# An RWKV-5 attention into a soft mixture of experts: K, R and V transposed as pairs of tokens, a shorter maximum, a reordered tail

## The chip, the cores and the metric

One core of one Trainium2 chip runs the whole program. The time is the device time of one execution, in microseconds (us). The kernel before took 127.64 us (median of 3 runs, 126.82 to 129.72).

## The reference

```python
B, H, S, D = 4, 8, 768, 48          # r, k, v: [B, H, S, D] fp32; w, u: [H, D]
for t in range(S):                  # attention with a decaying state
    cur   = einsum('bhd,bhe->bhde', u * k_t, v_t)
    y_t   = einsum('bhd,bhde->bhe', r_t, state + cur)
    state = w * state + einsum('bhd,bhe->bhde', k_t, v_t)
x = y.transpose(0, 2, 1, 3).reshape(3072, 384)
logits = x @ phi                    # phi: [384, 32], 8 experts of 4 slots
d = exp(logits - logits.max(0)); d /= d.sum(0)
slots = d.T @ x                     # [32, 384]
slot_out = relu(slots @ w1[e]) @ w2[e]     # per expert, w1 [384,1024], w2 [1024,384]
c = exp(logits - logits.max(1)); c /= c.sum(1)
out = c @ slot_out                  # [3072, 384] fp32
```

## The kernel before, in words

**Attention.** The recurrence is done in chunks of 128 tokens. K is multiplied by a table of w to powers, R by another, so that a chunk becomes a masked product of K and R times V, plus a state product between chunks. Work comes in 12 *tiles* (a third of a batch element, all heads; `J` = 8 consecutive tokens lie side by side in a partition) and 16 *units* (a batch element and a pair of heads, `e` = 0 and 1).

For each tile three loads (`load`, SP queue, 384 KB each) bring K, R and V into a ring `raw` of 7 slots of three tensors. `scale` then writes them as bf16 into `kr` (two buffers per tensor): K and R with a `tensor_mul` by the table `W` (line 207), V with a copy (line 205). Nearly all of this is done by GpSimd (POOL). `turn` (line 261) transposes each of the three with 8 TensorE transposes of 128x128 bf16 into one of three PSUM buffers `T`; `turned` copies `T` out with ScalarE (ACT) as `kT`, `rT`, `vT`. K and V are turned once more (kinds 3 and 4, giving `kn` and `vn`).

For each unit `a_pe` (line 294) forms the K-R products and VectorE (DVE) masks them (`mask_f`, line 299); `ds_pe` (323) and `m_pe` (316) form diagonal and state terms, `z_evac` and `dv_ev` take them out; `y_pe` (345, 352, 356) forms the outputs, and `y_evac` writes them into `x` on ACT for the units in `xact`, on DVE for the others. `xt` (377) transposes `x` for the logits.

**Experts.** Per batch element `lg_pe` (388) forms the logits. The maximum over the batch element is taken in five steps: `max_a` (maximum along the row, DVE), `max_b` (transpose, 395), `max_c` (maximum, DVE), `max_d` (broadcast by a matmul, 401), `max_e` (change of sign, DVE). `le_ev` takes the exponentials, `disp` (438) forms the slot inputs, `le_t` and `le_tev` (427, 431) keep the transposed exponentials `LexpT` for the end. After the last batch element the tail runs in the written order: W1 (708, with ReLU on ACT and DVE), transpose of the last exponentials, row and column sums (721, 725), transposes of the hidden values (732, copied at 733), W2 (737: 64 matmuls, group 0 and then group 1, whose last expert is number 7), scaling into `so` (747, 748), and 24 output matmuls (761) with their evictions (763, 765) and 8 output transfers (767).

**Weights.** `load_w` issues W1 (line 131, 8 transfers of 768 KB as written) and W2 (line 134, 7 and 2 halves) from POOL's queue, fp32 in memory and bf16 on chip. W2 goes into the space of `raw`. These issues stand in POOL's program between its `scale` instructions: the first W1 behind 16 of them, the eighth behind 32, and W2 behind the last one.

**Order.** The attention and the logits are put in order by a planner in the kernel (`Task`): it simulates the engines with fixed durations and priorities (`PR`) and emits instructions in the order of its own clock. Every engine executes its instructions in that order. `fill` and `keep_warm` are matmuls whose result nobody reads.

Of the kernel before, what the change touches and what calls it, by code (L numbers as in the profile page):

```python
# [9 lines left out]
def kernel(  # L10
# [51 lines left out]
    NS = 7  # L62
    RW = 2 * J * D
    SL = 3 * RW
    raw = big.tile([128, NS * SL], f32, name="raw")
# [3 lines left out]
    W2_OFF = [(2 * SL * (NS - 2) + e * eW2) if e < 3 else (e - 3) * eW2 for e in range(E)]  # L69
# [4 lines left out]
    def raw_of(which, t):  # L74
        o = (t % NS) * SL + which * RW
        return raw[:, o:o + RW]
# [10 lines left out]
    gb_p = Mb[:, 448:449]  # L87
    D_p = Ab[:, 0, 384:384 + (nM + 1) * ES]
    mx_p = Ab[0:1, 1, 384:512]

    LexpT = cst.tile([128, J, Nn // J], bf, name="LexpT")
    LexpT_f = LexpT[:].rearrange("p j x -> p (j x)")
# [16 lines left out]
    def load(t):  # L109
        b, x = divmod(t, nX)  # L110
        for which, src in ((0, k), (1, r), (2, v)):
            O(sp.dma_start(out=raw_of(which, t).rearrange("p (e f) -> p e f", e=2), in_=flat(src, b)[x]))

    load(0)
# [6 lines left out]
    for t in range(1, 4):  # L121
        load(t)
# [3 lines left out]
    for t in range(4, NS):  # L126
        load(t)
# [26 lines left out]
    O(pool.iota(tr_i, pattern=[[1, J], [J, R]], base=0, channel_multiplier=0))  # L154
# [32 lines left out]
    kr_t = [[cst.tile([128, J, 2, 64], bf, name=f"kr{w_}_{j}") for j in range(NK)] for w_ in range(3)]  # L187
    wuT = cst.tile([128, 8], f32, name="wuT")
    for w_ in range(3):
        O(dve.memset(kr_t[w_][0][:].rearrange("p j e s -> p (j e) s")[:, :, D:64], 0.0))  # L190
# [4 lines left out]
    for w_ in range(3):  # L195
        O(pool.memset(kr_t[w_][1][:].rearrange("p j e s -> p (j e) s")[:, :, D:64], 0.0))

    cast = {}

    def scale(t, w_, eng):  # L200
        b, x = divmod(t, nX)
        kr = kr_t[w_][t % NK][:].rearrange("p j e s -> p e j s")[:, :, :, 0:D]
        src = raw_of(w_, t).rearrange("p (e j d) -> p e j d", e=2, j=J)
        if w_ == 2:
            O(eng.tensor_copy(kr, src))  # L205
        else:
            O(eng.tensor_mul(kr, src, W[w_][:, x]))  # L207
        cast[t] = cast.get(t, 0) + 1
        if cast[t] == 3 and t + NS < nT:
            load(t + NS)  # L210

# [3 lines left out]
    one_f = cst.tile([1, 128], f32, name="one_f")  # L215
# [5 lines left out]
    g_row = cst.tile([1, 1], f32, name="g_row")  # L221
# [18 lines left out]
    def clear():  # L240
        O(pool.memset(ones[:], 1.0))
        O(pool.memset(one_f[:], 1.0))
        O(pool.memset(Le[:], 0.0))
        O(pool.memset(cs_f[:], 1.0))
        O(pool.memset(uns[:], 0.0))
# [10 lines left out]
    def turn(kind, t):  # L256
        st["bank", kind, t] = k_ = bank()
        src = None if kind < 3 else st["kT" if kind == 3 else "vT", t]
        for j in range(J):
            x_in = kr_t[kind][t % NK][:, j].rearrange("p e s -> p (e s)") if kind < 3 else src[:, j * C:(j + 1) * C]  # L260
            O(pe.transpose(T[k_][:, j * C:(j + 1) * C], x_in, ident[:]))  # L261

    def turned(kind, t):
# [7 lines left out]
        if kind == 3:  # L271
            O(act.copy(o[:].bitcast(f32), Tf[k_]))  # L272
        else:
            O(act.copy(o[:].bitcast(f32).rearrange("p (g j c) -> p g j c", g=J, j=J),  # L274
                       Tf[k_].rearrange("p (j g c) -> p g j c", g=J, j=J)))

    def product(t):
        st["pr", t] = pr = wk.tile([128, J * C], bf, name="pr", bufs=BUFS["pr"])
        O(dve.tensor_mul(pr[:].rearrange("p (g j c) -> p g j c", g=J, j=J),  # L279
                         T[st["bank", 1, t]][:].rearrange("p (j g c) -> p g j c", g=J, j=J),  # L280
                         st["kT", t][:].rearrange("p (g j c) -> p g j c", g=J, j=J)))
# [112 lines left out]
    def max_b(b):  # L394
        O(pe.transpose(mx_p, mx[:], ident_f[:]))

    def max_c(b):
        O(dve.tensor_reduce(out=g_row[:], in_=mx_p, axis=AX.X, op=ALU.max))

    def max_d(b):  # L400
        O(pe.matmul(gb_p, one_f[:], g_row[:], start=True, stop=True))

    def max_e(b):

        O(dve.tensor_scalar(out=ref[:, 1:2], in0=gb_p, scalar1=-1.0, scalar2=None, op0=ALU.mult))
# [22 lines left out]

    def le_tev(b):
        o = LexpT[:, :, b * nC * R:(b + 1) * nC * R].bitcast(f32).rearrange("p j (c x) -> p c j x", c=nC)  # L430
        O(act.copy(o, Tf[st["bank", "l", b]][:, 0:nC * C // 2].rearrange("p (c j x) -> p c j x", c=nC, j=J)))
# [16 lines left out]
    PR = {'lead': 0.88, 'tab': [0, 0.27, 3.9], 'kind': [0.08, 0.79, -0.38, 1.68, 0.93], 'pr': -0.37, 'A': -3.77, 'mask': 3.15, 'M': -1.24, 'dv': 3.1, 'Y': 1.22, 'xt': 4.4, 'rt': 2.58, 'w0': 36, 'slack': 0.05, 'dve_scales': [(1, 1)], 'xact': [0, 1, 2, 6, 10, 11, 14]}  # L448

    LAT = {"pe": 0.24, "act": 0.08, "dve": 0.08, "pool": 0.10}  # L450
    TURN, TURNED = 0.46, 0.59
    tasks, users = [], {}

    class Task:
        def __init__(self, eng, dur, prio, emit, deps=(), psum=None, after=0.0, takes=False, gives=None):
            self.eng, self.dur, self.prio, self.emit = eng, dur, prio, emit
            self.deps = [d for d in deps if d is not None]
            self.psum, self.after, self.takes, self.gives = psum, after, takes, gives
# [19 lines left out]
    tab = {}  # L478
    for x in range(1, nX):
        for j in range(2):  # L480
            m = Task("dve", 0.95, PR["tab"][x], lambda j=j, x=x: table_mul(j, x))
            tab[j, x] = Task("act", 0.80, PR["tab"][x], lambda j=j, x=x: table_exp(j, x), [m])
# [5 lines left out]
    for t in range(nT):  # L488
        x, u0 = t % nX, first_unit(t)
        for w_ in range(3):  # L490
# [5 lines left out]
            if x and t < nX and w_ < 2:  # L496
                deps.append(tab[w_, x])
            s_ = Task(eng, dur, 3 * t + w_ - 40, lambda t=t, w_=w_, e=eng: scale(t, w_, pool if e == "pool" else dve),
                      deps, after=4.3 + 1.07 * (3 * t + w_))
            s_.ring = [sc[t - NS, j] for j in range(3)] if t >= NS else []  # L500
            sc[t, w_] = s_
        for kind in range(5):
            p = u0 - LD + PR["kind"][kind]
            deps = [sc[t, kind]] if kind < 3 else [K["ev", 0 if kind == 3 else 2, t]]
            if (kind, t - 1) in K:
                deps.append(K[kind, t - 1])
            a = Task("pe", TURN, p, lambda k_=kind, t=t: turn(k_, t), deps, takes=True)
# [23 lines left out]
        for i in [i for i in range(nU) if tiles_of(i)[-1] == t]:  # L531
# [3 lines left out]
            for f in range(2):  # L535
                tf = tiles_of(i, f * L, f * L + L)
                a = Task("pe", 0.20, i + PR["A"] + 0.1 * f, lambda i=i, f=f: a_pe(i, f),
                         [K["ev", k_, t_] for k_ in range(2) for t_ in tf] + ([prev["A"]] if "A" in prev else []), psum="A")
# [4 lines left out]
                for t_ in tf:  # L543
                    uses(a, ("kT", t_), ("rT", t_))
            d = Task("pe", 0.16, i + PR["M"], lambda i=i: ds_pe(i),
                     [K["pr", t_] for t_ in tl] + [uc] + ([prev["dv"]] if "dv" in prev else []), psum="M")
            kv = Task("pe", 0.28, i + PR["M"], lambda i=i: m_pe(i),
                      [K["ev", k_, t_] for k_ in (3, 4) for t_ in tl] + [d] + ([prev["Z"]] if "Z" in prev else []), psum="M")
# [3 lines left out]
            for t_ in tl:  # L552
# [5 lines left out]
                     A + [z] + ([dv] if on_act else []) + ([prev["x"]] if "x" in prev else []), psum="Y")  # L558
# [10 lines left out]
            if q >= 1:  # L569
                mi = q - 1  # L570
                a = Task("pe", 0.50, i + PR["xt"], lambda b=b, mi=mi: xt(b, mi), [xe], takes=True)
# [5 lines left out]
            if q == nQ - 1:  # L577
# [4 lines left out]
                if last:  # L582
                    fine = [Task("pe", 0.33, o, lambda b=b: lg_pe(b, range(nM - 1)),
                                 [prev["xt", b, m_] for m_ in range(nM - 1)] + [prev["Z"]] + fine, psum="M")]
                    uses(fine[0], ("xT", b))
                lg = Task("pe", 0.17 if last else 0.5, o, lambda b=b, m0=nM - 1 if last else 0, n=2 if last else 0: (lg_pe(b, range(m0, nM)), fill(n)),
                          [prev["xt", b, m_] for m_ in range(nM)] + fine, psum="M")
                uses(lg, ("xT", b))
                c1 = Task("dve", 0.35, o, lambda b=b: max_a(b), [lg], psum="M")
                c2 = Task("pe", 0.2, o + 0.1, lambda b=b, n=2 if last else 0: (max_b(b), fill(n)), [c1, cl] + ([prev["x"]] if last else []), psum="A")  # L590
                c3 = Task("dve", 0.28, o + 0.1, lambda b=b: max_c(b), [c2], psum="A")
                c4 = Task("pe", 0.05, o + 0.2, lambda b=b, n=1 if last else 0: (max_d(b), fill(n)), [c3], psum="M")
                c5 = Task("dve", 0.15, o + 0.2, lambda b=b: max_e(b), [c4] + ([prev["ref"]] if "ref" in prev else []), psum="M")
# [3 lines left out]
                di = Task("pe", 0.62, o + 0.5, lambda b=b: disp(b), [le], psum="A")  # L597
# [6 lines left out]
                a = Task("pe", 0.34, o + 0.6, lambda b=b: le_t(b), [le], takes=True)  # L604
# [7 lines left out]
    for n in range(NW):  # L612
        deps = [wprev] if wprev else []
        if n >= E:
            e_ = min(n - E, E - 1)
            lo, hi = 2 * W2_OFF[e_], 2 * (W2_OFF[e_] + eW2)
            for t in range(nT):
                k_ = t % NS
                if t + NS >= nT and lo < (k_ + 1) * SL * 4 and hi > k_ * SL * 4:
                    deps += [sc[t, w_] for w_ in range(3)]  # L620
# [31 lines left out]

    done = []
    while todo:
# [13 lines left out]
        tk.start, tk.end = when, when + tk.dur  # L668
        at_eng[tk.eng] = tk.end + 0.03
# [13 lines left out]
    fill(3)  # L683
# [15 lines left out]
    PH = C // 2  # L699
    Wf = [t[:].rearrange("p x e j d -> p (x e j d)") for t in W]  # L700
# [3 lines left out]
    for g in range(2):  # L704
        for a in range(2):
            for mi in range(nM):
                for j in range(EG):
                    O(pe.matmul(hb[g][a][32 * j:32 * j + 32, 0:FH], uns[:, g, mi, j, :],  # L708
                                w1_all[:, g * EG + j, mi, a * FH:(a + 1) * FH],
                                start=(mi == 0), stop=(mi == nM - 1), skip_group_check=True))  # L710
# [32 lines left out]
    for j in range(EG):  # L743
        for y in range(nF):
            w2_mm(1, j, y)
# [52 lines left out]
```

## Time and profile before

| | |
|---|---|
| time of the profiled execution | 126.88 us |
| its span (first to last instruction) | 124.9 us |
| TensorE matmul (PE) | busy 101.2 us, 1912 instructions |
| TensorE weight load (PEld) | busy 76.1 us, 1913 instructions |
| DVE / ACT / POOL | busy 82.0 / 64.7 / 61.9 us |
| DMA share of 16 engines | 49.8% POOL's queue, 42.3% SP's queue |
| HBM | 39.38 MB read, 4.72 MB written |

PE and PEld overlap, so their busy times do not add. The TensorE clock was granted at 0.965 of full speed on average. Weights are written at half the bytes that are read, because the transfer casts them to bf16.

### The profile page before, as it was taken

What the parts mean: (1) busy time and instruction counts of PE and PEld (TensorE: products, weight loads), DVE (VectorE), ACT (ScalarE), POOL (GpSimd) and SP (SyncE); (2) the same over time, 40 slices, a digit from 0 to 9 for tenths busy, and PEclk for the clock granted to TensorE, in tenths of its full rate; (3) what the DMA queues carried; (4) which work ended last, traced back from release to release, by engine and by line L of the source; (5) the groups of instructions that cost most, each with busy time, mean ns of one, the idle gap of its engine ahead of it and who ended that gap; (6) DMA issues with size and microseconds to landing.
All of it is one profiled execution on the core that took longest, in us unless ns stands there. A gap on an engine that the chain in (4) does not pass through costs nothing.

```text
span 124.9 us, 4413 instructions
## 1 busy us (share of the span) xinstructions
PE 101.2 (81%) x1912; PEld 76.1 (61%) x1913; DVE 82.0 (66%) x139; ACT 64.7 (52%) x130; POOL 61.9 (50%) x70
## 2 busy tenths in 40 slices
PE   6998669999979899989799996976988989697000
PEld 2647557878868788867678885864774465442000
DVE  5896996638778795778598799676644442199000
ACT  4146986877566664766446664832631220199000
POOL 7612999999999999996397921000000000000000
PEclk9999999999999999999999999999779999999965
DMA  3999999999999999999999999999999950049992
GB/s 92 331 376 383 361 364 376 372 374 373 371 372 373 250 187 208 211 213 220 219 204 213 190 215 216 215 210 219 214 220 214 201 112 5 0 187 408 411 402 107
DMA packets 13863, 31.79 MB, mean 255 GB/s; under 512 B 1428, under 2 KB 10644, under 8 KB 13844
## 3 DMA queue, kind: packets, MB, share of 16 engines
q0 software_dynamic: 2448, 12.58, 49.8%
q1 hardware_dynamic: 11360, 18.93, 42.3%
q8 instruction: 15, 0.25, 0.8%
q14 instruction: 4, 0.03, 0.1%
q10 hardware_dynamic: 36, 0.00, 0.0%
HBM read 39.38 MB, written 4.72 MB: 353 GB/s over the span
## 4 chain that ended last, share of the span: by engine, by line
PE 53%; DVE 8%; issue 5%; ACT 4%; DVEq 0%; ACTq 0%
PE T L261 15%; PE Ab L294 5%; PE T L377 5%; DVE w_all L763 5%; PE Yb L345 4%; PE Mb L737 4%; PE Yb L352 3%; PE Mb L316 3%; PE Ab L438 2%; PE Mb L323 2%; PE Mb L388 2%; PE T L427 2%; PE Yb L356 1%; PE Yb L143 1%; PE T L708 1%
## 5 line engine op out<-in xcount | busy, mean ns | idle before, releaser
L207 POOL TENSOR_TENSOR kr<-raw,W 128x768 bf16<-128x768 f32 x21 | 37.8, 1815 | 4.4 <-issue 3.3
L299 DVE TENSOR_TENSOR AT<-Ab,mask_ut 128x768 bf16<-128x768 f32 x32 | 30.5, 953 | 7.0 <-PE Ab L294 5.9
L261 PE MATMUL T<-ident,kr 128*128 128x128 bf16 x288 | 22.0, 224 | 1.8 <-ACT Z L330 0.7
L261 PEld LDWEIGHTS <-kr 128*128 128x128 bf16 x288 | 17.6, 100 | 4.3 <-issue 1.2
L205 POOL CAST kr<-raw 128x768 bf16<-128x768 f32 x12 | 10.6, 886 | 5.8 <-DMA raw<-in_v_dram 5.8
L336 DVE TENSOR_TENSOR dv<-vn,Mb 128x576 bf16<-128x576 bf16 x16 | 11.9, 747 | 1.7 <-PE Mb L323 1.3
L294 PE MATMUL Ab<-rT,kT 64*128 64x128 bf16 x192 | 11.0, 219 | 1.6 <-DVE AT L299 1.1
L279 DVE TENSOR_TENSOR pr<-T,kT 128x1024 bf16<-128x1024 bf16 x12 | 8.2, 684 | 4.7 <-ACT rT L274 4.6
L382 ACT COPY xT<-T 128x384 f32<-128x384 f32 x12 | 5.8, 486 | 7.0 <-PE T L377 6.5
L377 PE MATMUL T<-ident,x 128*64 128x128 bf16 x144 | 7.0, 230 | 2.9 <-issue 2.8
L274 ACT COPY kT<-T 128x512 f32<-128x512 f32 x12 | 7.1, 593 | 3.6 <-PE T L261 3.5
L345 PE MATMUL Yb<-vn,AT 128*128 128x48 bf16 x192 | 7.7, 185 | 1.0 <-DVE W L180 1.0
L294 PEld LDWEIGHTS <-kT 64*128 64x128 bf16 x192 | 5.6, 94 | 4.6 <-issue 2.2
L274 ACT COPY vT<-T 128x512 f32<-128x512 f32 x12 | 7.1, 589 | 2.6 <-PE T L261 2.4
L366 ACT CAST x<-Yb 128x576 bf16<-128x576 f32 x7 | 4.5, 638 | 7.1 <-PE Yb L356 7.1
L274 ACT COPY rT<-T 128x512 f32<-128x512 f32 x12 | 7.1, 588 | 2.0 <-PE T L261 1.9
L261 PE MATMUL T<-ident,vT 128*128 128x128 bf16 x96 | 7.4, 219 | 0.8 <-ACT vT L274 0.8
L272 ACT COPY kn<-T 128x512 f32<-128x512 f32 x12 | 7.1, 594 | 1.7 <-PE T L261 1.6
L267 ACT COPY vn<-T 128x512 f32<-128x512 f32 x12 | 7.1, 592 | 1.4 <-PE T L261 1.4
L261 PE MATMUL T<-ident,kT 128*128 128x128 bf16 x96 | 7.5, 220 | 0.2 <-issue 0.2
L134 POOL DMA_DIRECT2D raw<-in_moe_w_dram x9 | 4.8, 558 | 5.3 <-DMA raw<-in_moe_w_dram 3.7
L330 ACT CAST Z<-Mb 128x240 bf16<-128x240 f32 x16 | 5.8, 365 | 3.0 <-PE Mb L316 2.5
(120 smaller groups left out, 184.5 us busy)
## 6 DMA issues: line engine op xcount, KB each, us to landing
w_all<-in_moe_w_dram POOLq DMA_DIRECT2D x8, 768.0 KB, 9.2
raw<-in_moe_w_dram POOLq DMA_DIRECT2D x7, 768.0 KB, 18.1
raw<-in_k_dram SPq DMA_DIRECT2D x12, 384.0 KB, 7.9
raw<-in_r_dram SPq DMA_DIRECT2D x12, 384.0 KB, 8.3
raw<-in_v_dram SPq DMA_DIRECT2D x12, 384.0 KB, 8.3
out_dram<-w_all SPq DMA_DIRECT2D x4, 768.0 KB, 5.6
out_dram<-w_all SPq DMA_DIRECT2D x4, 384.0 KB, 4.4
raw<-in_moe_w_dram POOLq DMA_DIRECT2D x2, 384.0 KB, 26.6
```

What stands on the lines that cost most here:

```text
L205: O(eng.tensor_copy(kr, src))
L207: O(eng.tensor_mul(kr, src, W[w_][:, x]))
L261: O(pe.transpose(T[k_][:, j * C:(j + 1) * C], x_in, ident[:]))
L267: O(act.copy(vn[:, x * J:(x + 1) * J].rearrange("p g e s -> p (g e s)").bitcast(f32), Tf[k_]))
L272: O(act.copy(o[:].bitcast(f32), Tf[k_]))
L274: O(act.copy(o[:].bitcast(f32).rearrange("p (g j c) -> p g j c", g=J, j=J), Tf[k_].rearrange("p (j g c) -> p g j c", g=J, j=J)))
L279: O(dve.tensor_mul(pr[:].rearrange("p (g j c) -> p g j c", g=J, j=J), T[st["bank", 1, t]][:].rearrange("p (j g c) -> p g j c", g=J, j=J), ...
L294: O(pe.matmul(Ab[:, e, (c - f * L) * C:(c - f * L + 1) * C], st["kT", t][s, sl], st["rT", t][s, sl]))
L299: O(dve.tensor_mul(AT[:], Ab[:, :, 0:L * C].rearrange("p e (c t) -> p e c t", c=L), mask_ut[:, None, None, :].to_broadcast([128, 2, L, C])))
L336: O(dve.tensor_mul(dv[:], vn[:, q * nC:(q + 1) * nC, :, 0:D].rearrange("p c e d -> p e c d"), ds_p.rearrange("p (c e) -> p e c", e=2)[:, : ...
L345: O(pe.matmul(Yb[:, e, c * D:(c + 1) * D], AT[c // L][:, e, c % L, :], vn[:, kap, e, 0:D], start=(c == 0), stop=(c == 0), skip_group_check ...
L377: O(pe.transpose(T[k_][64 * e:64 * e + 64, c * C:(c + 1) * C], x[:, c, f0:f0 + 64], ident[:]))
```

## The change

- `kr` holds, for each channel, its 8 tokens side by side, so that two bf16 tokens form one 4-byte word. `scale` writes 2-byte values 16 bytes apart. `turn` transposes K, R and V as 4 fp32 transposes of 128x128 in place of 8 bf16 ones; its stationary operand steps 16 bytes. Kinds 3 and 4 stay as they are.
- `LexpT` pairs tokens in the same way; `tokens(i)` picks every second one.
- The maximum: `max_b` becomes an fp32 matmul of the broadcast row maxima with minus the identity, `max_c` a minimum over its 128 columns on all partitions; `max_d` and `max_e` go.
- `raw` is a ring of 19 single tensors; each `scale` issues the load 19 tensors on. W2 lies in the slots of tensors 17 to 32.
- A tile of 128 bytes ahead of `raw`: `raw` and `w1_all` start at 16640 and 75008 bytes in the partition, before at 16512 and 81024.
- The planner counts TensorE's instructions and holds a task back where 256 more come within 5.95 us. Its other constants are new, too; 9 units are evicted by ACT in place of 7.
- The tail: the last `le_t` comes ahead of the slot inputs, the first hidden transpose ahead of the last W1 part, `so` is one DVE instruction, and 12 fills of 512 columns stand within W2's second group.

```diff
-    NS = 7
+    NS = 19
-    raw = big.tile([128, NS * SL], f32, name="raw")
+    big.tile([128, 32], f32, name="pad")
+    raw = big.tile([128, NS * RW], f32, name="raw")
...
-    kr_t = [[cst.tile([128, J, 2, 64], bf, name=f"kr{w_}_{j}") ...
+    kr_t = [[cst.tile([128, 2, 64, J], bf, name=f"kr{w_}_{j}") for j in range(NK)] for w_ in range(3)]
+    kr_f = [[t[:].rearrange("p e s j -> p (e s j)").bitcast(f32).rearrange("p (x g) -> p x g", g=HJ) for t in ts]
+            for ts in kr_t]
...
     def scale(t, w_, eng):
-        kr = kr_t[w_][t % NK][:].rearrange("p j e s -> p e j s")[:, :, :, 0:D]
+        dst = kr_t[w_][t % NK][:, :, 0:D, :].rearrange("p e d j -> p e j d")
...
-        if cast[t] == 3 and t + NS < nT:
-            load(t + NS)
+        if n + NS < 3 * nT:
+            load(n + NS)
...
     def turn(kind, t):
-        for j in range(J):
-            x_in = kr_t[kind][t % NK][:, j].rearrange("p e s -> p (e s)") if kind < 3 else ...
-            O(pe.transpose(T[k_][:, j * C:(j + 1) * C], x_in, ident[:]))
+        if kind < 3:
+            for g in range(HJ):
+                O(pe.transpose(Tf[k_][:, g * C:(g + 1) * C], kr_f[kind][t % NK][:, :, g], ident_f[:]))
+        else:
...
     def max_b(b):
-        O(pe.transpose(mx_p, mx[:], ident_f[:]))
+        O(pe.matmul(mx_p, mx[:].to_broadcast([128, 128]), neg_f[:], start=True, stop=True))
     def max_c(b):
-        O(dve.tensor_reduce(out=g_row[:], in_=mx_p, axis=AX.X, op=ALU.max))
-    def max_d(b):
-        O(pe.matmul(gb_p, one_f[:], g_row[:], start=True, stop=True))
-    def max_e(b):
-        O(dve.tensor_scalar(out=ref[:, 1:2], in0=gb_p, scalar1=-1.0, scalar2=None, op0=ALU.mult))
+        O(dve.tensor_reduce(out=ref[:, 1:2], in_=mx_p, axis=AX.X, op=ALU.min))
...
+        if tk.ni:
+            n_pe += tk.ni
+            if n_pe >= 256:
+                n_pe -= 256
+                past = when + tk.dur * (tk.ni - n_pe) / tk.ni
+                begun = max(past, begun + FETCH)
+                tk.end += begun - past
...
-    fill(3)
+    le_t(B - 1)
+    le_tev(B - 1)
+    fill(1)
...
+    w1_mm(0, 0)
+    w1_mm(0, 1)
+    w1_mm(1, 0)
+    h_turn(0)
+    w1_mm(1, 1)
...
     for j in range(EG):
+        if j == EG - 2:
+            fill(6)
         for y in range(nF):
+            if j == EG - 1 and y % (nF // 2) == 0:
+                fill(3)
             w2_mm(1, j, y)
     so = cst.tile([128, Dm], bf, name="so")
-    O(dve.tensor_scalar_mul(so[:, 0:Dm // 2], SO[:, 0:Dm // 2], csr[:]))
-    O(act.activation(out=so[:, Dm // 2:Dm], in_=SO[:, Dm // 2:Dm], func=AF.Copy, scale=csr[:]))
+    O(dve.tensor_scalar_mul(so[:], SO, csr[:]))
```

In the order of the instructions the change leaves POOL's weight issues where they were, behind 16 to 32 `scale` instructions, and SP's loads in the order of the tensors but for one exchange. TensorE's list, counted with a weight load for each matmul, falls from 3826 to 3556.

## Prediction, made before the changed kernel ran

> **What bounds the kernel now.** I read the chain of work that ended last first, then counted instructions between its pauses, then asked what feeds the last stage. Through the attention the chain stays on TensorE, and its pauses are "issue", time in which the engine waited for nothing that the profile shows:
>
> ```profile
> 53.26 0.10 PE T L427
> 53.35 0.50 issue
> ...
> 58.90 0.17 PE T L377
> 59.07 0.98 issue
> ...
> 76.32 0.23 PE T L377 x4
> 76.55 0.99 issue
> ```
>
> The pauses cut through groups of transposes that wait for no one. In the stretches from one restart to the next, the windows count (columns: length, then PE busy and count, PEld busy and count, DVE, ACT, POOL):
>
> ```profile
> 42.01:47.66 5.65, 5.49 (x128) 4.61 (x128) 5.10 (x8) 3.28 (x7) 5.63 (x6) 1.00 1.02 202
> 47.66:53.85 6.19, 5.69 (x128) 4.76 (x128) 3.95 (x9) 3.87 (x9) 6.17 (x7) 1.00 1.03 210
> 53.85:60.05 6.20, 5.21 (x128) 4.42 (x128) 5.04 (x7) 3.35 (x7) 4.96 (x5) 1.00 1.03 214
> ```
>
> Each stretch holds 128 matmuls and 128 weight loads: 256 instructions, whatever they do. The restarts at 35.54, 42.01, 47.66, 53.85, 60.05, 65.42, 71.50, 77.54 and 83.74 are 6.02 us apart on average. The page has a queue for this:
>
> ```profile
> q8 instruction: 15, 0.25, 0.8%
> ```
>
> 15 packets of 16 KB are 15 times 256 instructions of 64 bytes, and the list has 3826. In the trace a packet starts 2.7 to 3.9 us after a restart, takes about 1 us, and TensorE goes on 1.3 to 1.6 us after its end: 6 us for 256 instructions. So TensorE is held by the supply of its instructions. The matmuls on both sides of these pauses start 0.92, 0.75, 0.37, 0.72, 1.22, 0.28, 1.21 and 1.07 us apart where 0.06 is usual: about 6.1 us lost. The Trainium skill ("Runtime: NRT & Kernel Launch", Instruction fetch mechanics) has the same 256-instruction blocks but calls the cost of a boundary mostly hidden; by that rule fewer instructions would gain nothing here and the sum would lose its largest term. The rows above decide against it.
>
> Last I looked at what the end waits for. The transfers of the weights:
>
> ```profile
> 97.50:103.20 5.70, 4.94 (x96) 3.14 (x95) 2.51 (x7) 1.68 (x3) 0.00 (x0) 1.00 0.75 147
> 103.20:108.10 4.90, 4.77 (x64) 2.93 (x65) 0.63 (x3) 0.00 (x0) 0.00 (x0) 1.00 0.01 3
> ```
>
> The DMA share (next to last column) is full until the last half of W2's expert 7 lands at 103.14; the 64 W2 matmuls run from 103.27 to 108.06. So there is a second bound 5 us below the first: a faster TensorE meets the weights.
>
> **The change part by part.** Times are of the profiled execution: 126.88 us, of which 124.9 is the span and 2.0 lies around it; the median of the runs is 0.8 higher.
>
> *Fewer instructions.* 36 turns lose 8 each. At the last `disp` the list stands at 3116 where it stood at 3406: 290 fewer, 1.13 blocks. Between 35.54 and 83.74 us stand 2048 instructions, 168 pairs of them in 21 turns; the change takes 168 out and leaves 1880. If the supply still sets the pace, 48.2 us become 48.2 x 1880/2048 = 44.25: -4.0. If it no longer did, all 6.1 would go. I take -4.5, with -0.5 for the one stall ahead of that stretch (0.92 at 34.6, block by block the same) and ends at -4.0 and -6.1. Both bounds then lie close together: the work within a block, 6.02 - 0.76 = 5.26 us, grows by 2048/1880 to 5.73, just under the 6.02.
>
> *What an fp32 turn costs TensorE.* Eight bf16 transposes take 0.45 to 0.55 us in the chain (56 ns from start to start). No chain of fp32 transposes is in the trace, only single ones:
>
> ```profile
> L261 PE MATMUL T<-ident,kr 128*128 128x128 bf16 x288 | 22.0, 224 | 1.8 <-ACT Z L330 0.7 <-POOL ucol L236 0.5 <-POOL kr L205 0.3
> L721 PE MATMUL Ab<-ident_f,cs_f 128*128 128x128 f32 x1 | 0.3, 278 | 0.0
> L721 PEld LDWEIGHTS Ab<-ident_f,cs_f 128*128 128x128 f32 x1 | 0.1, 140 | 0.0
> ```
>
> In L721 the matmul starts 54 ns after its weight load. From below: the load hides behind the matmul ahead, as in bf16: 4 x 56 = 0.24 us. From above: the load isn't hidden and its 16-byte steps double it, to the 106 ns between the two loads of one fp32 matmul in line 401: 4 x (106 + 56) = 0.65. Nearest is L721, load and stream one after the other: 4 x (54 + 56) = 0.44, as before. I take 0; the ends are 36 x -0.21 = -7.6 and 36 x +0.20 = +7.2 us of TensorE work.
>
> *POOL writes 2 bytes at 16-byte steps.* The rows before:
>
> ```profile
> L207 POOL TENSOR_TENSOR kr<-raw,W 128x768 bf16<-128x768 f32 x21 | 37.8, 1815 | 4.4 <-issue 3.3 <-PE T L261 0.8
> L205 POOL CAST kr<-raw 128x768 bf16<-128x768 f32 x12 | 10.6, 886 | 5.8 <-DMA raw<-in_v_dram 5.8
> ```
>
> An element costs 2.4 ns with two inputs and 1.1 with one; a contiguous memset of 768 bf16 (line 243) takes 727 ns, 0.95 an element, so POOL seems to write element by element already, and the step may not matter. Below: 0 (nothing gets shorter). Above: nothing in the trace scatters so; I let a cast rise to the two-input row, +0.9 each, and the two-input row by half. I take 0 as likeliest, since the writes are no denser than before, and give the rest to two rivals. The Trainium skill ("GPSIMD Engine Reference", Performance pitfalls for Q7 kernels) speaks against the change: reads at steps beyond 8 bytes cost half as much again. It says so of reads, and no run here shows it for writes; if writes followed it, the sum would be that of the third rival below.
> This cover matters because POOL carries the weight issues: it's busy 24.6 of the 25.0 us from 12.66 to the first W1 issue at 37.63, and 24.0 of 27.4 to the eighth at 65.05. What is queued behind a slower `scale` is W1, then W2, then the end. The loads on SP are reissued per tensor, so a slot comes free no later than before; 19 slots for 21 are hidden by the queue, which holds 8 transfers ahead.
>
> *Maximum.* Last round: from 94.32 (transpose) to 95.63 (exponential) 1.31 us. Now one fp32 matmul in two passes (about 0.45 from the 133 ns between passes of line 401 and a 0.27 end), a minimum as before (0.28), two hops (0.1): 0.83. -0.5. The three earlier rounds lie beside other TensorE work: 0.
>
> *Tail.* From W1's start (97.53) to the first W2 matmul 5.74 us: W1 2.71, the transpose and copy of the exponentials 1.0, sums 0.75, hidden transposes 0.48, copy 0.74. Now W1 2.71, first hidden transpose 0.46 within it, sums 0.75 (they hide the last ReLU, 0.69), second transpose 0.46: 4.4. -1.35. The exponentials' transpose moves ahead (+0.4) in place of two fills (-0.43). W2 then takes 4.8 and the 12 fills 12 x 0.213 = 2.6 (0.65 for 3, as before `uns`). W2's end on TensorE's path: 108.06 - 4.5 - 0.5 - 1.35 + 2.6 = 104.3. On the weights' path: the landing at 103.14, 4 more matmuls and hops, 0.5: 103.6. The later one sets it, and 104.3 has room to fall by up to 1.6 (the stalls' other end) until the weights take over: I take 104.0, -4.1.
> `so` is one instruction of 0.61 in place of 0.43 + 0.43 and a hop: -0.3.
>
> *256-byte starts.* A load's packet of 1536 B takes 66 ns (43 ns a KB), one of 6144 B of the outputs 236 (38): at most 11% of 36 x 1.045 us, -4.1; at least 0. The first W1 issue waits for POOL, not for the loads, so little of it can reach the end: 0 to -2 there, 0 to -0.8 in the outputs (12.9 us of transfer). I take -0.2.
>
> The output stage keeps its 24 evictions and 8 transfers. The 2 more ACT evictions (0.64 each) lie in ACT's idle third. Sum: -4.1 - 0.3 - 0.2 = -4.6: 122.3 us on the profiled execution's base, which I keep.
>
> **Rivals.** (1) *TensorE gets dearer*: the strided fp32 load isn't hidden, 0.65 a turn. The stalls vanish (-6.1), the turns add 7.2, fills 2.6, tail and maximum -1.85: +1.8, less 0.5: 128.2. For it: the 140 ns load; against: L721 shows 54, and its operand lacked only the step. (2) *Casts alone get slower*, by 0.55: 11 of them behind 12.66 add 6 us to POOL; the eighth W1, which could go at 12.66 + 24.6 + 24.0 = 61.3 without waits, goes at 67.3, and the end of W2 comes 38.1 later (as from 65.05 to 103.14) plus 0.5: 105.9. 124.2. (3) *All of POOL slows, and the kernel is slower than before*: `scale` fills 43.9 us up to the eighth W1. At 1.20 times its duration that issue comes at 70 and the gain is gone; at 1.26 the kernel is 2% slower; at 1.5, 83.3 + 38.1 + 0.5 = 121.9 for W2's end: 140. Against: 2.4 ns an element leaves room for a write. (4) *Everything falls*: turns at 0.24 and loads in time, weights landing 2 us earlier, outputs 0.8 shorter: W2's end 101.6, 119.3. (5) *The supply shrinks with it*: a block takes longer than 6.02 when its instructions last longer, so no stall goes: 126.9. Against: the block's time didn't follow its content (5.37 to 6.47 at equal counts).
>
> **How the numbers follow.** Forecast 0.52, (1) 0.09, (2) 0.16, (3) 0.10, (4) 0.10, (5) 0.03. The range 118.8 to 127.6 takes in (2), (4), most of (1)'s lower half and leaves (3) out. The measurement tells about 2% from no change (125.1 to 130.2). Faster: the forecast, (4), and two thirds of (2): 0.73. Same: the rest of (2), (1) less its dearest part, (5): 0.14. Slower: (3) and that part: 0.13.
>
> **What would show it.** Right: 256-instruction stretches still near 6 us but fewer; the last `disp` near 91; 4 fp32 transposes in 0.45 us or less; POOL rows at 1815 and 886 within 5%; TensorE idle or filling before the last W2 half, landing near 103. Wrong: a POOL row above 2000 or a cast above 1300, the first W1 issue later than 39, or fp32 starts over 130 ns apart.

## The result, and the profile after

The changed kernel takes 188.88 us (median of 4 runs, 187.5 to 190.1) against 127.61 us before: 1.482 times as long (95% interval 1.470 to 1.494). Some executions of one and the same kernel run a few per cent longer at a lower granted clock; the ratios in this document leave these out, the medians in us count them. The forecast was 122.3, with a range up to 127.6. What came is the prediction's third rival, at a price far beyond the one it was given.

The groups on POOL and TensorE, after (columns as before: busy us, mean ns of one, idle time ahead and who ended it):

```profile
L214 POOL TENSOR_TENSOR kr<-raw,W 128x768 bf16<-128x768 f32 x21 | 76.7, 3850 | 0.4 <-POOL ucol L243 0.3
L212 POOL CAST kr<-raw 128x768 bf16<-128x768 f32 x12 | 52.3, 4392 | 2.0 <-DMA raw<-in_v_dram 2.0
```

```profile
L265 PE MATMUL T<-ident_f,kr 128*128 128x128 f32 x144 | 34.9, 393 | 42.3 <-POOL kr L212 32.4 <-DVE kr L214 5.5 <-POOL kr L214 4.4
```

The same values with the same operations: 3850 ns where 1815 were, 4392 where 886 were, 129.0 us of POOL where 48.4 were (sums of the two groups; some records overlap, and with each moment counted once POOL's work on `kr` covers 124.0 us in place of 49.1). And TensorE, which hardly waited for POOL before, now stands idle for 42.3 us ahead of its turns. The page's slices show the same two things, POOL at 80% or more in 28 of 40 slices, and the granted TensorE clock down to half in between:

```profile
POOL 8599899999999999999999999999911000000000
PEclk9999955579575769759685887969579999999965
```

The chain that ended last (columns: start, length, what) runs over POOL to its last `scale` and its weight issues, then over TensorE to the end:

```profile
122.23 5.73 POOL kr L214 x2
127.96 0.99 issue
128.95 0.59 POOL w_all L133
...
129.54 3.64 POOL kr L212
...
133.22 1.98 PE T L265 x8
...
162.96 1.01 PE Mb L754 x21
163.98 8.27 issue
172.25 0.63 DVE so L780
```

The 8.27 us of "issue" at the end are DVE's, while the W2 matmuls run. The 63.4 us by which the span grew (124.9 to 188.3) add up so: the first W2 issue, which stands behind the last `scale` on POOL, goes from 68.17 to 132.72, +64.6; from there to the last `disp` it takes 23.6 in place of 27.9, -4.3; from that `disp` to the end of W2 15.8 in place of 12.0, +3.9; the outputs 16.1 in place of 16.8, -0.7.

The windows show TensorE slow while POOL works and full again once it is done (last columns: granted clock, DMA share, GB/s):

```profile
60.00:80.00 20.00, 12.34 (x170) 10.26 (x168) 7.10 (x9) 6.52 (x13) 19.98 (x8) 0.76 0.23 51
...
140.00:150.00 10.00, 9.35 (x241) 7.36 (x238) 7.02 (x9) 5.60 (x13) 0.54 (x1) 1.00 1.04 214
```

Even the DMA, saturated through the attention before, has a share of 0.23 here: loads wait for slots, weights for POOL.

### The profile page after: what moved, and what is told of

Its sections match the earlier page's. It is cut to its first block, busy times and chain, and to the rows that moved or that the text cites. A ratio compares the mean times of both kernels' runs of the same rounds, so it can differ in the third digit from the quotient of the medians.

```text
span 188.3 us, 4152 instructions
## 1 busy us (share of the span) xinstructions
PE 129.9 (69%) x1776; PEld 94.4 (50%) x1778; DVE 93.0 (49%) x132; ACT 67.9 (36%) x132; POOL 133.9 (71%) x70
## 5 line engine op out<-in xcount | busy, mean ns | idle before, releaser
L214 POOL TENSOR_TENSOR kr<-raw,W 128x768 bf16<-128x768 f32 x21 | 76.7, 3850 | 0.4 <-POOL ucol L243 0.3
L265 PE MATMUL T<-ident_f,kr 128*128 128x128 f32 x144 | 34.9, 393 | 42.3 <-POOL kr L212 32.4
L212 POOL CAST kr<-raw 128x768 bf16<-128x768 f32 x12 | 52.3, 4392 | 2.0 <-DMA raw<-in_v_dram 2.0
L265 PEld LDWEIGHTS T<-ident_f,kr 128*128 128x128 f32 x144 | 24.8, 217 | 47.5 <-POOL kr L212 34.3
L214 DVE TENSOR_TENSOR kr<-raw,W 128x768 bf16<-128x768 f32 x3 | 14.8, 5050 | 0.0
L303 PE MATMUL Ab<-rT,kT 64*128 64x128 bf16 x192 | 13.2, 255 | 1.0 <-DVE AT L308 1.0
L269 PE MATMUL T<-ident,kT 128*128 128x128 bf16 x96 | 10.4, 273 | 0.0
L377 DVE TENSOR_TENSOR x<-Yb,dv 128x576 bf16<-128x576 f32 x7 | 5.3, 755 | 9.0 <-PE Yb L361 9.0
L269 PEld LDWEIGHTS <-kT 128*128 128x128 bf16 x96 | 8.3, 125 | 1.0 <-issue 0.5
L797 ACT ACTIVATE w_all<-T,rsr 128x384 f32<-128x384 f32 x8 | 4.3, 603 | 12.2 <-PE T L793 12.2
```

Of the source, the lines that this page charges most:

```text
L212: O(eng.tensor_copy(dst, src))
L214: O(eng.tensor_mul(dst, src, W[w_][:, t % nX]))
L265: O(pe.transpose(Tf[k_][:, g * C:(g + 1) * C], kr_f[kind][t % NK][:, :, g], ident_f[:]))
L269: O(pe.transpose(T[k_][:, j * C:(j + 1) * C], src[:, j * C:(j + 1) * C], ident[:]))
L303: O(pe.matmul(Ab[:, e, (c - f * L) * C:(c - f * L + 1) * C], st["kT", t][s, sl], st["rT", t][s, sl]))
```

## Experiments

Theory W: the scattered 2-byte writes alone make `scale` slow, and the rest follows. Rival T: the fp32 turns have a share. Rival R: ring, order or tail lose it. A second question came up on the way, where the gain of the other parts went.

**Two halves of the change.** `layout_only` is the kernel before with only the new `kr`, its turns and the paired tokens; `rest_only` is the changed kernel with these put back.

```diff
 # rest_only, against the changed kernel (the paired order of tokens put back with it)
-        dst = kr_t[w_][t % NK][:, :, 0:D, :].rearrange("p e d j -> p e j d")
+        dst = kr_o[w_][t % NK].rearrange("p j e s -> p e j s")[:, :, :, 0:D]
...
-                O(pe.transpose(Tf[k_][:, g * C:(g + 1) * C], kr_f[kind][t % NK][:, :, g], ident_f[:]))
+                O(pe.transpose(T[k_][:, j * C:(j + 1) * C], kr_o[kind][t % NK][:, j].rearrange("p e s -> p (e s)"), ident[:]))
```

> The kernel before with only the new kr layout, its fp32 turns and the token order that follows. Theories W and T: 183 to 193 us, nearly the whole loss. Rival R: under 140.

Measured: 1.485 times before (1.469 to 1.500). The POOL rows are those of the changed kernel, 3848 and 4340 ns.

> The changed kernel with before's kr layout, its eight bf16 transposes a turn and its token order; ring, maximum, tail, fills, start lines and order settings as changed. Theories W and T, which both put the loss into the new layout: 123 to 127 us (127.6, less 0.5 for the maximum and 1.35 for the tail, the stalls of instruction supply still there, fills beside the weights). Rival R (the ring per tensor, the order or the tail holds the weights back): above 140, first W1 issue still late (over 50 us).

Measured: 1.004 (0.996 to 1.011); 128.27 us, first W1 issue at 37.20. So the layout is the whole loss and R falls. But the other parts, with which 123 to 127 us had been expected, gain nothing either; more on that below.

**Writes without turns, turns without writes.** `dense_write` writes 48 values without a gap as before and turns 4-byte words at 16-byte steps; `scatter_bf` writes as the change does and turns dense bf16 columns. Both leave out the order of the values, so they compute something else with the same instructions.

```diff
 # dense_write
-        dst = kr_t[w_][t % NK][:, :, 0:D, :].rearrange("p e d j -> p e j d")
+        dst = kr_o[w_][t % NK].rearrange("p j e s -> p e j s")[:, :, :, 0:D]
 # scatter_bf
-                O(pe.transpose(Tf[k_][:, g * C:(g + 1) * C], kr_f[kind][t % NK][:, :, g], ident_f[:]))
+                O(pe.transpose(T[k_][:, j * C:(j + 1) * C], kr_o[kind][t % NK][:, j].rearrange("p e s -> p (e s)"), ident[:]))
```

> The changed kernel, scale writing before's dense pieces of 48 values into the same tiles while the turns still read 4-byte words at 16-byte steps; the decay tables are set to one (the same instructions) and the order of the values is left out. Theory W with cheap turns: first W1 issue at 37 to 39 us, POOL rows at 1815 and 886, 121 to 124 us in all. Theory W with turns of 0.85 us each (36 times 0.4 more, 6 us of stalls gone): 128 to 137. Theory T alone (turns hold POOL through the two kr buffers): above 165, W1 still late, with POOL idle in between.

> The changed kernel with its scattered writes kept and only the turns put back to eight bf16 transposes of dense columns of the same tiles; the decay tables are set to one (the same instructions) and the order of the values is left out. The other half of the pair with dense_write. Theory W (the writes alone): 184 to 194 us, first W1 issue still at 75 to 80. Theory T (the fp32 turns have a share): under 175.

Measured: `dense_write` 0.992 (0.986 to 0.999), 126.66 us, above the 121 to 124 expected (the fills, below, account for this), first W1 issue at 36.65; `scatter_bf` 1.488 (1.477 to 1.499), first W1 issue at 77.44. The groups of `dense_write`, then of `scatter_bf`:

```profile
L216 POOL TENSOR_TENSOR kr<-raw,W 128x768 bf16<-128x768 f32 x21 | 37.9, 1822 | 4.4 <-PE T L267 3.2 <-POOL kr L214 0.8 <-ACT W L186 0.2
L214 POOL CAST kr<-raw 128x768 bf16<-128x768 f32 x12 | 10.9, 904 | 3.8 <-DMA raw<-in_v_dram 3.8
...
L267 PE MATMUL T<-ident_f,kr 128*128 128x128 f32 x144 | 25.5, 311 | 0.4 <-DVE pr L290 0.4
```

```profile
L216 POOL TENSOR_TENSOR kr<-raw,W 128x768 bf16<-128x768 f32 x21 | 76.5, 3836 | 0.3 <-POOL ucol L245 0.3
L214 POOL CAST kr<-raw 128x768 bf16<-128x768 f32 x12 | 51.2, 4304 | 2.9 <-DMA raw<-in_v_dram 2.9
```

The writes decide, whatever the turns are: W stands, and T has no share that can be told. The fp32 transposes of `dense_write` start 0.122 us apart (median), those of the changed kernel 0.213. The changed kernel has both paces: 213 ns where its bf16 transposes start 107 apart (36 to 38 us, granted clock 0.50), 121 where they start 56 apart (near 90 us). It is TensorE's pace that halves, not a price of the fp32 form.

**The instruction by itself.** `micro` and `micro2` time instructions one engine after the other, with nothing else going on.

```python
O(pool.tensor_copy(b_old, s3))     # line 133: before's output
O(pool.tensor_mul(b_old, s3, w3))  # 135
O(pool.tensor_copy(b_step, s3))    # 137: after's output, 2 bytes at 16-byte steps
O(pool.tensor_mul(b_step, s3, w3)) # 139
O(pool.tensor_copy(b_in, s3.rearrange("p e j d -> p e d j")))   # 141: dense writes, reads at 192-byte steps
O(pool.tensor_mul(b_in, s3.rearrange("p e j d -> p e d j"), w3.rearrange("p e j d -> p e d j")))   # 143
```

> Not the kernel: single instructions timed one engine after the other, the rest of the work left out. Theory W (writes of 2 bytes at 16-byte steps are slow by themselves): on POOL the copy and the two-input instruction with after's output take 3.4 us or more alone, against 0.9 and 1.8 with before's output; DVE's too (over 4 against 1.2). Within W, if the distance counts, the cost rises in the steps 2, 4, 8, 16, 32 bytes, and 4-byte words at 16-byte steps are as slow; if the 2-byte piece of a word counts, a step of 4 bytes is already slow and 4-byte words at any step are fast. Rival C (contention: DMA, DVE and POOL meet in the memory): alone after's form takes no more than 1.2 times before's. Theory T (turns): 16 fp32 transposes in a row start 0.21 us apart whatever the step of their operand if the four-byte passes cost it, and 0.11 with a dense operand if the step costs it; bf16 ones 0.056.

> Not the kernel: copies of 768 values timed one after the other, the rest of the work left out; the same six steps for 2-byte outputs (2 to 64 bytes) and five for 4-byte outputs (4 to 64 bytes). So far 2-byte outputs took 826, 1037, 1884, 3584 and 3384 ns at 2, 4, 8, 16 and 32 bytes, 4-byte ones 928, 872 and 1541 at 4, 8 and 16. Theory N (the number of values skipped counts, whatever their size): 4-byte outputs take 3.3 to 3.7 us at 32 bytes, as 2-byte ones do at 16. Theory H (writing half a word costs twice): 4-byte outputs level off at half of the 2-byte ones, 1.6 to 1.9 us at 32 bytes and beyond.

POOL's groups of `micro`:

```profile
L139 POOL TENSOR_TENSOR d_b<-rw,wt 128x768 bf16<-128x768 f32 x2 | 7.2, 3596 | 0.2
...
L137 POOL CAST d_b<-rw 128x768 bf16<-128x768 f32 x2 | 7.2, 3584 | 0.1
...
L143 POOL TENSOR_TENSOR d_b<-rw,wt 128x768 bf16<-128x768 f32 x2 | 5.5, 2757 | 0.2
...
L135 POOL TENSOR_TENSOR d_b<-rw,wt 128x768 bf16<-128x768 f32 x2 | 3.6, 1802 | 0.2
...
L141 POOL CAST d_b<-rw 128x768 bf16<-128x768 f32 x2 | 2.9, 1466 | 0.1
...
L133 POOL CAST d_b<-rw 128x768 bf16<-128x768 f32 x2 | 1.7, 826 | 14.1 <-DVE rw L122 14.1
```

Alone, too, a copy rises from 826 to 3584 ns and two inputs from 1802 to 3596: no contention is needed, rival C falls. In the kernel the same instructions took somewhat more (3850 and 4392 ns); what adds these 7 and 23% was not tested. DVE's copy, at 1868 ns, stays far below the 4 us expected of it; its two-input form takes 3558. On POOL both end at the same figure, 4.67 ns a value, so the write sets it and the arithmetic hides behind it. All steps, 768 fp32 values in, mean ns of one instruction (both kernels; the dense fp32 copies, 928 and 658 here, took 830 and 560 in `micro2`):

| output, distance of the values | 2 B | 4 B | 8 B | 16 B | 32 B | 64 B |
|---|---|---|---|---|---|---|
| POOL copy to bf16 | 826 | 1037 | 1884 | 3584 | 3384 | 3513 |
| POOL two inputs to bf16 | 1801 | 1805 | 1910 | 3596 | 3428 | |
| ACT copy to bf16 | 830 | 1044 | 1893 | 3588 | 3396 | 3522 |
| DVE copy to bf16 | 544 | 595 | 1020 | 1868 | 1774 | 1917 |
| DVE two inputs to bf16 | 958 | 1009 | 1862 | 3557 | 3382 | |
| POOL copy to fp32 | | 928 | 872 | 1541 | 1558 | 1468 |
| DVE copy to fp32 | | 658 | 562 | 847 | 858 | 849 |

```profile
L157 POOL COPY d_w<-rw 128x768 f32<-128x768 f32 x2 | 3.1, 1558 | 0.1
L155 POOL COPY d_w<-rw 128x768 f32<-128x768 f32 x2 | 3.1, 1540 | 0.1
```

These two are `micro2`'s 4-byte outputs at 32 and 16 bytes. They level off at 1.9 to 2.0 ns a value, the 2-byte ones at 4.4 to 4.7: theory H, writing half a word costs over twice as much (1558 ns is just under its 1.6 to 1.9 us), and N falls. That holds from 8-byte steps on; at 4 bytes a 2-byte copy takes 1037 ns, near the 928 of a dense 4-byte one. Both level off from 16 bytes on, and at 8 bytes a 2-byte value costs half of that, at 4 bytes a quarter and a bit: the figures fit one price for each 16 bytes touched. The Trainium skill ("SBUF — State Buffer", Door 1: The DMA port swizzle) states lines of 16 bytes, with a penalty for each access that goes to a new line; the knee at 16 bytes agrees. It adds that 8 bf16 can be strided for free; here a step of 8 values took POOL's copy to 4.3 times its dense time, and the measurement decides. Its "Vector Engine (DVE) Microarchitecture Reference" (5.2 Measured stream behaviour on trn2) has up to 2.51 ns a value where 4-byte outputs alone step, by 24 words. Here DVE's two-input form took 1.98 with 4-byte outputs at 16 bytes (1520 ns for 768) and 4.63 with 2-byte ones.

TensorE in `micro`, at a granted clock of 1.00: bf16 transposes start 56 ns apart, dense fp32 ones 109, fp32 ones at 16-byte steps 120. Theory T's 0.21 us doesn't occur here; the step adds 11 ns.

**Other ways through the pairs.** `jinner` keeps the layout and swaps the loops, so that writes are dense and reads step 192 bytes.

```diff
-        dst = kr_t[w_][t % NK][:, :, 0:D, :].rearrange("p e d j -> p e j d")
-        src = raw_of(n).rearrange("p (e j d) -> p e j d", e=2, j=J)
+        dst = kr_t[w_][t % NK][:, :, 0:D, :]
+        src = raw_of(n).rearrange("p (e j d) -> p e d j", e=2, j=J)
```

> The changed kernel, its scale walking through the pairs in another order: the 2-byte writes now follow each other without gaps, and the reads of raw and of the tables go in steps of 192 bytes. Alone such instructions took 1466 (copy) and 2757 ns (two inputs), 1.55 times before's mix. If POOL's time for scale sets the end, as in the prediction's third rival: eighth W1 issue near 85 us and 137 to 146 us in all. If it is the scattering as such and not POOL's time: back to 126 to 130. If order of any kind is as bad as the scattered write: above 175.

Measured: 1.198 (1.186 to 1.210), 151.44 us, above the range. The rows are dearer in the kernel than alone (2757 and 1466):

```profile
L214 POOL TENSOR_TENSOR kr<-raw,W 128x768 bf16<-128x768 f32 x21 | 60.1, 2887 | 0.4 <-POOL ucol L243 0.3
L212 POOL CAST kr<-raw 128x768 bf16<-128x768 f32 x12 | 20.6, 1715 | 3.2 <-DVE kr L214 2.9 <-DMA raw<-in_v_dram 0.2
```

80.7 us for 48.4 are 1.67 times. The prediction's sum for its third rival, 83.3 us for the eighth W1 issue at 1.5 times, gives 83.3 + 0.17 x 43.9 = 90.8 with this; measured 93.40, and the last half of W2 landed 37.9 us later, at 131.31, where 38.1 had been taken. The path from POOL's time to the landing of the weights is right; its input was wrong. W2 ended 1.8 us after the landing, at 133.07, where 0.5 had been taken: its stage started at 123.81 and took 9.26 us with the fills.

`pair4_nofill` lays the pairs as dense 4-byte words, so that the writes step 4 bytes; it needs two instructions a tensor, and leaves out the fills, whose story follows.

```diff
-    kr_t = [[cst.tile([128, 2, 64, J], bf, name=f"kr{w_}_{j}") for j in range(NK)] for w_ in range(3)]
+    kr_t = [[cst.tile([128, HJ, 2, 64, 2], bf, name=f"kr{w_}_{j}") for j in range(NK)] for w_ in range(3)]
...
+        for e in range(2):
+            dst = kr_t[w_][t % NK][:, :, e, 0:D, :].rearrange("p g d w -> p g w d")
```

> The changed kernel with its pairs kept, but the 4-byte words of a pair lying densely (64 words for each pair of tokens, then the next pair): scale writes 2 bytes at 4-byte steps, in two instructions of 384 values each, turns read dense fp32 words; no fills between the W2 matmuls. Alone a copy at this step took 1037 against 826 ns, two inputs 1805 against 1801, and dense fp32 transposes start 109 ns apart (120 at 16-byte steps). Theory W with the step as its cause: POOL 1.05 to 1.15 times before's time for scale, eighth W1 issue at 66 to 70, the last W2 half at 103 to 107: 123.5 to 127.5 us. If writing half a word is slow in itself: above 140.

Measured: 0.987 (0.975 to 0.998), 125.71 us. The step is the cause: the pairs cost little at 4 bytes, and half a word is not slow to write in itself. Two instructions take 2 x 1035 and 2 x 655 ns, so POOL needs 55.9 us for 48.4, the first W1 issue goes at 40.47, and the last half of W2 lands at 106.67 (103.10 in the run of the same kind with before's `kr`, `rest_nofill_b`).

**Where the rest's gain went.** In `rest_only` the last `disp` starts at 92.36 (96.10 before) and the first W2 matmul at 98.94 (103.27 before), yet W2 ends at 108.19 as before (108.05).

```diff
 # rest_nofill, against rest_only
     for j in range(EG):
-        if j == EG - 2:
-            fill(6)
         for y in range(nF):
-            if j == EG - 1 and y % (nF // 2) == 0:
-                fill(3)
             w2_mm(1, j, y)
```

> rest_only without the 12 fills between the W2 matmuls. In rest_only the W2 stage starts 4.3 us earlier than before and ends at the same 108.0. Theory F (the fills lie on the path: 12 of 0.215 us each, and they part the pairs of experts that before ran side by side): W2 ends 0.7 to 1.0 us after the last half lands, 104.0 to 104.5, and 123.5 to 125 us in all. Rival K (the fills keep TensorE's clock and pay for themselves): the granted clock falls below 1.00 in the stage, W2 ends at 107 or later, 127 to 129.

Measured: 0.967 (0.960 to 0.974), 122.59 us, below the range. Once more, as `rest_nofill_b`:

> The same kernel as rest_nofill, once more for a narrower interval and for the profile of an ordinary execution: 0.96 to 0.975 of before, W2 ending at 104 to 104.5 us.

Measured: 0.969 (0.967 to 0.971), 122.82 us; W2 ends at 104.19, 1.1 after the last half lands. TensorE's and DVE's groups in the W2 stage, in `rest_only` and then in `rest_nofill_b`:

```profile
L753 PE MATMUL Mb<-raw,W 128*32 128x384 bf16 x64 | 6.6, 327 | 0.0
...
L145 PE MATMUL Yb<-vn,ident 128*128 128x512 bf16 x11 | 2.9, 381 | 0.2 <-issue 0.2
...
L779 DVE TENSOR_SCALAR so<-Mb,csr 128x384 bf16<-128x384 f32 x1 | 0.6, 618 | 8.3 <-issue 8.3
```

```profile
L753 PE MATMUL Mb<-raw,W 128*32 128x384 bf16 x64 | 4.8, 327 | 0.0
...
L775 DVE TENSOR_SCALAR so<-Mb,csr 128x384 bf16<-128x384 f32 x1 | 0.6, 618 | 3.8 <-issue 3.8
```

Each matmul lasts the same, but the 64 cover 6.6 us in place of 4.8: without fills the matmuls of one expert start in pairs with those of the next (0.163 us for two), and the fills part the experts. With their own 2.9 the stage takes 9.25 in place of 4.77. The granted clock is 1.00 with and without them: theory F stands, K falls.

`dense_nofill` is `dense_write` without the fills:

> dense_write without the 12 fills (the decay tables set to one and the order of the values left out, as there): what the change would be if its writes cost nothing and nothing was put between the W2 matmuls. In dense_write the first 48 W2 matmuls ended at 102.1 and the last half landed at 103.06: W2 ends at 103.7 to 104.3 here, 122 to 123.5 us, no better than rest_nofill because the weights end last in both. If the fp32 turns still help or hurt by more than the weights hide: a ratio to rest_nofill outside 0.99 to 1.01.

Measured: 0.957 (0.950 to 0.963), 121.96 us, 1.2% better than `rest_nofill_b` and just outside the 0.99 to 1.01: with writes at no cost the fp32 turns help a little. The last `disp` starts at 90.31, the W2 stage then waits 1.35 us for its last half (landing at 103.21) and ends at 104.06. So with writes at no cost and no fills the change would have taken about the 122.3 us forecast, but that is luck: the terms behind it differ, as the part on the prediction shows.

**What brings the attention's end forward by 3 us.** `rest_only` gains 3.7 us there, of which only the maximum's 0.5 was a term of the prediction. Four runs put one part back each, and a fifth, `before_pad`, adds one alone:

```diff
 # nopad_nofill, against rest_nofill; before_pad adds the same line to before
-    big.tile([128, 32], f32, name="pad")
 # oldring_nofill: 21 slots, three reloaded together
-        if n + NS < 3 * nT:
-            load(n + NS)
+        if cast[t] == 3 and t + 7 < nT:
+            for j in range(3):
+                load(3 * (t + 7) + j)
```

`oldorder_nofill` takes before's constants and no account of instruction supply, `oldmax_nofill` the maximum in five steps.

> rest_nofill with before's order settings and without the planner's account of instruction supply, so that the instructions of the attention come in another order. In rest_only the last disp starts at 92.4 us where it started at 96.1 before. Theory O (the order gives these 3.7 us): the last disp at 95 to 96, W2 ends at 106.5 to 107.5, 125 to 127 us. Rival G (ring, maximum and 256-byte starts give them): disp near 92.4, 122 to 123.5 us.

> rest_nofill with the 128 bytes ahead of raw taken out, so that raw and W1 start 128 bytes past a multiple of 256, as before. Theory P (the start lines feed the attention earlier): raw loads follow each other at 1.04 us again instead of 0.97, TensorE's instruction 1473 comes 2 to 3 us later than 44.1, the last disp at 95 to 96, W2 ends at 106.5 to 107: 124.8 to 126 us. Rival Q (the ring per tensor does it, or the maximum): 122.3 to 123.3.

> The kernel before with nothing but the 128 bytes ahead of raw. Theory P: raw loads 0.97 us apart, the last disp at 93 to 94 instead of 96.1, W2 ends at 105 to 106 since no fills lie in its way: 0.975 to 0.985 of before. Rival Q: 0.995 to 1.005.

> rest_nofill with before's maximum in five steps. If the maximum gives the attention's 3 us (four rounds of two steps and hops fewer, 0.5 us each, none of it hidden): the last disp at 94.5 to 95.5 instead of 92.85, 124.3 to 125.5 us. If the ring does: 0.5 us for the last round alone, hidden by the weights for the most part, 122.5 to 123.4.

> rest_nofill with before's raw ring: 21 slots, three of them reloaded together once the third is cast. If the ring gives the 3 us: the last disp at 95 to 96, 124.5 to 126 us. If the maximum does: 122.5 to 123.4.

| run | to before (95%) | last `disp` |
|---|---|---|
| rest_nofill_b | 0.969 (0.967 to 0.971) | 92.85 |
| oldorder_nofill | 0.963 (0.958 to 0.967) | 92.82 |
| nopad_nofill | 0.979 (0.973 to 0.986) | 93.11 |
| oldmax_nofill | 0.973 (0.968 to 0.978) | 94.90 |
| oldring_nofill | 0.973 (0.968 to 0.978) | 93.00 |
| before_pad | 0.996 (0.990 to 1.002) | not read: its profiled execution took 132.4 us |

None of the four is it alone. Starts on 256 bytes are worth some 1% in the good version, where the prediction had -0.2 us, 0.7 us of it in the outputs (16.8 us after W2's end in the profile without, 16.1 in the one with them). They are worth nothing that can be told in the kernel before, though the raw loads do come 0.97 us apart in place of 1.05. Maximum and ring give some 0.4% each, within their intervals. The new order shows no gain: the 0.963 without it rests on two of six executions, and the median of all six is 123.97 us against 122.82. The 94.90 of `oldmax_nofill` comes from an execution of 124.40 us where the median is 123.45, so it does not show 2 us for the maximum. Otherwise the last `disp` moves by 0.3 us or less, so the parts put back one at a time do not add up to the 3 us. What gives the rest was not tested, and single executions spread: before's own ran from 125.6 to 132.6 us in these comparisons. How the 3 us divide stays open.

## Why the prediction was wrong

**POOL's scatter, taken at 0: the step that failed.** From 2.4, 1.1 and 0.95 ns an element the prediction concluded that "POOL seems to write element by element already, and the step may not matter." The inference from time to mechanism was wrong: a copy costs 1.1, 1.4, 2.5 and 4.7 ns a value at steps of 2, 4, 8 and 16 bytes by the table, so the dense price was one that neighbouring values share. Both upper ends failed, too: a cast rose by 2.76 us alone (3.5 in the kernel) where +0.9 us was the bound, the two-input row to 2.0 times alone (2.1 in the kernel) where 1.5 was. They were taken from rows that all wrote densely, and no row of before bore on scattered writes; an honest upper bound for something no row resembles would have had to be far wider, and the third rival more than 0.10. The prediction weighed a page of the Trainium skill on reads ("GPSIMD Engine Reference", Performance pitfalls for Q7 kernels: half as much again beyond 8 bytes) and not the one on 16-byte lines. The rule on reads holds with two inputs, which rose by 53% alone at 192-byte steps; a copy rose by 77%.

**The third rival's sum.** At the measured 2.67 times (129.0 / 48.4) it gives 83.3 + 1.17 x 43.9 = 134.7 for the eighth W1 issue, where 128.95 was measured, and 172.8 for the last half of W2; that landed at 166.89, 37.9 after the eighth W1. The factor counts overlapping records twice, which makes the sum too long. On the other side, W2 ended 5.3 us after the landing, at 172.15, where 0.5 had been taken, because its stage with the fills took 9.26 us from 162.89; in `layout_only`, without these fills, it ended 0.85 after (167.84). That the end comes out near is two deviations that cancel. The mechanism was on record, with the right chain up to the landing; its factor was mis-sized.

**Fp32 turn, 0.44 us, net 0.** Measured in `dense_write`: 0.64 from the start of a turn to the next group, against 0.55 for eight bf16 ones in `rest_only` (means, pauses included; medians 0.59 and 0.54). That is 1.7 (medians) to 3.1 us (means) for 36 turns, inside the ends of 0.24 and 0.65. The sign "fp32 starts over 130 ns apart" came true in the changed kernel for another reason than the one it was written for: 213 ns are TensorE at half its pace, waiting for POOL between turns.

**Fewer instructions, -4.5.** In `rest_only` TensorE still goes on after every 128 matmuls and 128 weight loads, some 6 us apart; in `dense_write` two such blocks took 12.73 us with TensorE busy throughout:

```profile
45.21:51.68 6.47, 5.82 (x128) 4.92 (x128) 4.47 (x9) 3.11 (x6) 5.83 (x6) 1.00 1.01 196
51.68:57.60 5.92, 5.70 (x128) 4.62 (x128) 5.16 (x8) 3.38 (x7) 5.88 (x6) 1.00 1.02 204
57.60:63.61 6.01, 5.80 (x128) 4.75 (x128) 4.46 (x6) 3.89 (x9) 4.43 (x5) 1.00 1.05 215
```

```profile
50.12:62.85 12.73, 12.73 (x255) 10.69 (x256) 9.67 (x13) 7.89 (x17) 9.07 (x9) 1.00 1.03 210
```

The pauses at block boundaries between 35 and 92 us (matmuls over 0.25 us apart) sum to 5.0 us in `rest_only` and 2.6 in `dense_write`, so 2.4 went, and the turns took 1.7 to 3.1: the last `disp` at 91.82 against 92.36. In `dense_nofill` it came at 90.31, near the 91 forecast, but by luck: 3.7 us of the way from 96.10 are the gain of the other parts, and the pairs themselves brought 0.5 us there (`dense_write` against `rest_only`) to 2.5 (`dense_nofill` against `rest_nofill_b`). That TensorE is held by its instruction supply is confirmed, the size was 2.1 too high.

**Maximum, -0.5**: 0.91 us in `rest_only` from the matmul's start to the exponential's (1.11 in `dense_write`) where 1.31 was, -0.4 to -0.2. **Tail, -1.35**: from the start of W1 to the first W2 matmul 5.31 us in `rest_only` (93.63 to 98.94), 5.81 before by the same reading (97.46 to 103.27); only -0.5.

**Fills, +2.6, and "I take 104.0".** W2 ended at 107.96 in `dense_write`, not at 104.3 or before. Its first matmul came at 98.70 where the working has 104.3 - 4.8 - 2.6 = 96.9: 0.7 from the last `disp`, 1.1 from the tail. Its stage took 9.26 where 7.4 stood: the fills' own time was right (2.9 with their gaps), but the W2 matmuls were held at 4.8 and took 6.6. That the fills come after the weights they should cover, and so lie on the path, is in the prediction's sum; that they part the experts is not. The bound by the weights held where no fills stood: the last half landed at 103.10 in `rest_nofill_b` and 103.21 in `dense_nofill`, and W2 ended 1.1 and 0.9 later. But the prediction read its row wrongly there: a DMA share of 0.75 is not full, and from 102.0 to 103.2 it was 0.11.

## What to carry to other kernels

Price the output's step before the input's: halving the transposes was paid with an output whose every value touches 16 bytes of its own, and on POOL and DVE that cost more than a second input did (a copy with such an output 3584 and 1868 ns, two inputs written densely 1802 and 958). Values of 2 bytes may step 4 bytes on POOL for nothing with two inputs (1805 against 1801 ns) and for a quarter more in a copy; at 8 a copy takes over twice as long, at 16 over four times. Where TensorE works in separate column groups, as in W2, matmuls put in between two runs cost the overlap, too (6.6 us for 4.8). The better version here is simply the changed kernel with before's `kr` and without the fills: 0.969.

## What the runs showed of the hardware

A 2-byte write costs 4.4 to 4.7 ns a value from 16-byte steps on, a 4-byte write 1.9 to 2.0, on POOL and ACT alike; DVE's copy takes about half of either (2.4 and 1.1), its two-input form 4.4 to 4.6 for 2 bytes and 2.0 for 4. Reads at 192-byte steps cost POOL 1.9 ns a value in a copy. In the changed kernel, where TensorE stood idle for 32.4 us in 11 waits for the V copy, the granted clock was 0.76 on average from 60 to 80 us. Where it was 0.50 (36 to 40 us), transposes started 107 (bf16) and 213 ns (fp32) apart, where it was full (near 90 us) 56 and 121, so a cadence read there says nothing of the instruction until the clock beside it is read. That the idling lowers the clock is not shown by a run of its own.
